# Two widths for the expert products: a branch on the expert's number of tokens chooses 224 or 256 columns

## The chip, the cores and the metric

The kernel runs on one core of one Trainium2 chip. The metric is the device time in microseconds (us) of one execution. TensorE's rows are named PE in the profile (PEld is its weight load), VectorE's DVE, ScalarE's ACT, GpSimd's POOL, and SyncE's SP. A "q" behind an engine's name marks its sequencer, the part that reads the program and hands instructions to the engine.

## The reference, cut to what matters

```python
def _moe_ref(x, w_gate, w1, w2, capacity):       # x: 1536 tokens of 512, from an attention
    expert_idx = np.argmax(x @ w_gate, axis=1)   # one of 8 experts for each token
    ...                                          # disp[e]: the tokens of expert e, capacity 384
    h = np.maximum(np.einsum('ecd,edf->ecf', disp, w1), 0.0)   # 512 -> 1024
    y = np.einsum('ecf,efd->ecd', h, w2)                       # 1024 -> 512
    ...                                          # out[i] = gate_w[i] * y[expert, position]
# reference: attention -> x -> _moe_ref -> SwiGLU of 512 -> 1536 -> 512
```

With the inputs that the reference draws, computing it gives 198, 119, 169, 188, 162, 192, 206 and 302 tokens for the experts 0 to 7.

## The kernel before

Three stages follow each other: the attention with the router (to about 284 us), the experts (to about 498 us), and the SwiGLU. The change is in the experts, in the class `Experts`.

`run` goes over the eight experts. The tokens of an expert are gathered as rows into `xr` by a DMA that ACT issues an expert ahead (the first by SP). `xt` turns two tiles of 128 tokens by transposes on TensorE (L839, tile `xp`) into `X`, 256 columns: a high part `Xh` (ACT, L842) and a rest `Xl` (DVE, L843). All products are made of such pairs, in three matmuls: high by high, high by rest, rest by high.

`l1` is called four times per expert. Each call fills one PSUM tile `hp` with 2 x 12 = 24 matmuls (L850) and evicts it: ACT writes `Hhh` with a Relu (L859), DVE the rest `Hhl` (L860). `l2` is called twice per expert; each call is 2 x 24 = 48 matmuls into `yp`, evicted to `Yh` (L870) and `Yl` (L871) at the column offset of the expert, which the engines hold in a register. An expert has so 4 x 24 + 2 x 48 = 192 matmuls, each with a weight load of its own; every one moves 256 columns, whatever the number of tokens.

An expert with more than 256 tokens has a third tile, in `over`, under a branch that all engines take by the register `cnt`; each engine loads it once per expert (L938), and the branch (L951) stands between the fourth `l1` and the transposes of the next expert:

```python
            cnt = ld(1, max_val=rt.CP) if nt > 2 else None
            ...
            for t in range(2, nt):
                with tc.If(cnt > t * 128):
                    self.over(e, t, off[t])
```

The order of the work on each engine is the order in the program. The weights come through four buffers `raw` (L807, SP's queue); `split` turns each into a high part (ACT, L816) and a rest (DVE, L817), in front of the calls of `l1` and `l2`. PSUM holds two `hp` and two `yp`, so that a product runs while the one before is evicted. Ahead of the first expert, 28 matmuls into an unused tile (L934) fill TensorE while the first rows are on their way; the first twelve of these have 192 columns.

Of the kernel before, what the change touches and what calls it, by code (L numbers as in the profile page):

```python
# [10 lines left out]
F32 = mybir.dt.float32  # L11
# [3 lines left out]
AF = mybir.ActivationFunctionType  # L15
ALU = mybir.AluOpType
# [749 lines left out]
class Experts:  # L766
# [43 lines left out]
    def split(self, e, i):  # L810
# [6 lines left out]
        nc.vector.tensor_tensor(out=l, in0=t, in1=h.bitcast(F32), op=ALU.subtract)  # L817
        self.load(8 * e + i + NRAW)

# [23 lines left out]
            nc.vector.tensor_tensor(out=X[1][:, ks, 0:n], in0=ps[:, :, 0:n], in1=X[0][:, ks, 0:n].bitcast(F32),  # L843
                                    op=ALU.subtract)

    def prod(self, out, W, ks, cols, mov):
        n, i = len(ks) * 3, 0
        for k in ks:
            for a, b in ((0, 0), (0, 1), (1, 0)):
                self.nc.tensor.matmul(out, lhsT=W[a][:, k, cols], rhs=mov[b][:, k, :], start=i == 0, stop=i == n - 1)  # L850
                i += 1

    def l1(self, mp, Hh, tag):
        nc = self.nc
        ps = self.ps.tile([128, 2, 256], F32, tag=tag, name="hp")
        for m in range(2):
            self.prod(ps[:, m], self.W1, range(self.KD), slice((2 * mp + m) * 128, (2 * mp + m + 1) * 128), self.X)
        ms = slice(2 * mp, 2 * mp + 2)
        nc.scalar.activation(out=Hh[0][:, ms], in_=ps, func=AF.Relu)  # L859
        nc.vector.scalar_tensor_tensor(out=Hh[1][:, ms], in0=ps, scalar=0.0, in1=Hh[0][:, ms].bitcast(F32), op0=ALU.max,  # L860
                                       op1=ALU.subtract)

    def l2(self, dp, Hh, off, n, tag):
        nc = self.nc
        ps = self.ps.tile([128, 2, 256], F32, tag=tag, name="yp")
        for m in range(2):
            self.prod(ps[:, m], self.W2, range(self.KF), slice((2 * dp + m) * 128, (2 * dp + m + 1) * 128), Hh)
        dsl = slice(2 * dp, 2 * dp + 2)
        y = [t[:, dsl, ds(off, n)] for t in self.Y]
        nc.scalar.copy(out=y[0], in_=ps[:, :, 0:n])  # L870
        nc.vector.tensor_tensor(out=y[1], in0=ps[:, :, 0:n], in1=y[0].bitcast(F32), op=ALU.subtract)  # L871

    def high_first(self, ks):

# [36 lines left out]
    def run(self, hook):  # L911
        nc, tc, rt = self.nc, self.tc, self.rt
        E, nt = self.E, self.nt
        ET = mybir.EngineType
        base = list(range(min(2, nt)))
        nb = 128 * len(base)
        if nb < 256:
            for t in self.X:
                nc.vector.memset(t.bitcast(F32), 0.0)
        self.rows(0, nc.sync)  # L920
        for k in range(self.KD):
            for t in self.Y:
                nc.gpsimd.memset(t[:, k].bitcast(F32), 0.0)
        for i in range(4):
            self.split(0, i)
        w = self.ps.tile([128, 2, 256], F32, tag="hp", name="hp").rearrange("p a b -> p (a b)")
        for i in range(14):
            nc.tensor.transpose(w[:, 0:128], self.ident, self.ident)
        rt.offsets(self.p1, self.ps.tile([128, 2, 256], F32, tag="xp", name="xp")[:, 0, 0:E])
        for i in range(24):  # L930
            nc.tensor.transpose(w[:, 0:128], self.ident, self.ident)
        for i in range(28):
            n = 512 if i > 11 else 192
            nc.tensor.matmul(w[:, 0:n], lhsT=self.W1[0][:, 0, 0:128], rhs=self.W1[0][:, 0, 0:n], start=True, stop=True)  # L934
        self.xt(0, base, "xp")
        for e in range(E):
            self.rows(e + 1)
            ld = lambda t, **k: nc.values_load(rt.offi[0:1, t, e:e + 1], min_val=0,  # L938
                                               skip_runtime_bounds_check_because="counts of tokens", **k)
            two = [ET.Activation, ET.DVE]  # L940
            off = {t: ld(t, engines=two, max_val=rt.N) for t in [0] + list(range(2, nt))}
            cnt = ld(1, max_val=rt.CP) if nt > 2 else None
            if e == 5:
                rt.hots([h[:, f] for h in self.Ho for f in range(self.KF)][:rt.B * rt.J], self.hs[:, 0:128])
            for mp in range(4):
                self.split(e, 4 + mp)
                self.l1(mp, self.Hh, "hp")
                if (e, mp) == (5, 3):
                    rt.tokens(self.ps.tile([128, 512], F32, tag="ov", name="xp")[:, 0:2 * rt.B * rt.J])
# [3 lines that stand above are left out]
            if e == 0:  # L953
                rt.ranks(self.p1)
                rt.invert(self.p1)
            if e + 1 < E:
                self.xt(e + 1, base, "xp")
            for dp in range(2):
                if e + 1 == E and dp:
                    hook(1)  # L960
                self.split(e + 1, 2 * dp)
                self.split(e + 1, 2 * dp + 1)
                if e + 1 == E and not dp:
                    hook(0)
                self.l2(dp, self.Hh, off[0], nb, "yp")
        hook(2)


class Glu:
# [51 lines left out]
    def convert(self, g, i):  # L1021
# [10 lines left out]
        v.scalar_tensor_tensor(out=b, in0=Hw, scalar=0xC0000000, in1=b, op0=ALU.bitwise_and, op1=ALU.bitwise_or)  # L1032
        v.scalar_tensor_tensor(out=m, in0=m, scalar=TINY, in1=b.bitcast(F32), op0=ALU.is_ge, op1=ALU.mult)  # L1033
        h, l = [w[:, i * 512:(i + 1) * 512] for w in self.sets[g % 2]]
        nc.scalar.copy(out=h, in_=m)  # L1035
        nc.gpsimd.tensor_tensor(out=l, in0=m, in1=h.bitcast(F32), op=ALU.subtract)  # L1036
        self.load(6 * g + i + NRAW)

# [72 lines left out]


NRAW = 4
TINY = 3.4332275390625e-05


@with_exitstack
def tile_clustered_attention_moe_swiglu(ctx, tc, q, k, v, cent, gate, w1, w2, wg, wv, wo, out, cap):
# [5 lines left out]
    const = ctx.enter_context(tc.tile_pool(name="const", bufs=1))  # L1124
    raw = ctx.enter_context(tc.tile_pool(name="rawp", bufs=NRAW))
    with tc.manual_schedule():
# [15 lines left out]
        with ExitStack() as c2:  # L1142
# [7 lines left out]
            with ExitStack() as c3:  # L1150
                ex = Experts(tc, c3, rt, w1, w2, ident, raw, W1, W2, Y)
                ex.next = glu.load
                for i in range(NRAW):
                    ex.load(i)
# [7 lines left out]
def dbg_attn(ctx, tc, q, k, v, cent, gate, xo, cap):  # L1162
# [4 lines left out]
    const = ctx.enter_context(tc.tile_pool(name="const", bufs=1))  # L1167
    raw = ctx.enter_context(tc.tile_pool(name="rawp", bufs=NRAW))
    with tc.manual_schedule():
# [41 lines left out]
```

## Time and profile before

| | |
|---|---|
| three runs | 803.13 us (median), 802.59 to 803.83 |
| the profiled execution | 802.74 us; span of its instructions 801.0 us |
| mean granted clock of TensorE | 0.995 of 2.4 GHz |
| PE busy | 776.8 us, 97% of the span |
| DVE, ACT, POOL busy | 529.3, 387.8, 191.8 us |
| matmuls with their weight loads | 4793 |

The profile is of one execution. A share of busy time near 100% says that an engine has something in hand, not that it runs at its best rate: matmuls overlap, so the distance between two starts counts, not the length of one. PEclk is the granted share of the TensorE clock: 1.0 is 2.4 GHz, 0.5 is 1.2 GHz. All times in rows are us from the start of the span.

### The profile page before, as it was taken

The numbers are of one execution on the slowest core, as the hardware profiler recorded it, in microseconds if no ns is written. First come the engines' busy times: TensorE is split into PE (matmuls) and PEld (weight loads), VectorE is DVE, ScalarE is ACT, GpSimd is POOL, SyncE is SP. The second block draws the span as 40 slices with busy tenths as digits, with TensorE's granted clock in tenths as the row PEclk, the third lists the DMA queues.
The fourth block names the chain that finished last, engine by engine and source line by source line (L and its number), as shares of the span: only waits on it lengthen the run. The fifth ranks groups of instructions, "written<-read, shape, count | busy, mean of one in ns | idle before, by whom it ended". The sixth has DMA issues, their size and how long they took to land. (4 is left out here: it accounts for less than half of the span.)

```text
span 801.0 us, 12679 instructions
## 1 busy us (share of the span) xinstructions
PE 776.8 (97%) x4793; PEld 652.8 (81%) x4793; DVE 529.3 (66%) x871; ACT 387.8 (48%) x704; POOL 191.8 (24%) x212
## 2 busy tenths in 40 slices
PE   7999999999999989999999999999999999999996
PEld 6777777777767789999999988778888888888885
DVE  5777777877877647565665644787766766676433
ACT  5777677777777535454554443354232232222210
POOL 6121121111211360000040001344333233323234
PEclk9999999999999989999999999999999999999999
DMA  9856966735541276656765641223121122210012
GB/s 203 198 119 198 220 173 180 178 81 118 139 155 40 80 262 198 196 192 211 234 202 191 194 126 54 82 99 109 54 80 52 55 78 66 66 54 1 0 53 105
DMA packets 93313, 102.03 MB, mean 127 GB/s; under 512 B 30304, under 2 KB 77408, under 8 KB 93248
## 3 DMA queue, kind: packets, MB, share of 16 engines
q1 hardware_dynamic: 88384, 89.33, 39.3%
q0 software_dynamic: 1920, 6.29, 2.1%
q10 hardware_dynamic: 2944, 5.54, 2.0%
q8 instruction: 41, 0.67, 0.3%
q14 instruction: 24, 0.20, 0.1%
HBM read 68.21 MB, written 12.58 MB: 101 GB/s over the span
## 5 line engine op out<-in xcount | busy, mean ns | idle before, releaser
L342 DVE TENSOR_REDUCE nm<-s 128x1 f32<-128x768 f32 x96 | 91.0, 949 | 12.1 <-PE s L339 10.5
L352 ACT ACTIVATE P<-s,nm 128x768 f32<-128x768 f32 x96 | 86.5, 901 | 13.4 <-DVE nm L342 10.4
L368 PE MATMUL t<-ident,P 128*128 128x128 f32 x576 | 81.2, 274 | 0.9 <-ACT PT L371 0.6
L368 PEld LDWEIGHTS t<-ident,P 128*128 128x128 f32 x576 | 68.5, 141 | 7.7 <-DVE PT L373 2.5
L850 PE MATMUL hp<-Xl,W1h 128*128 128x256 f32 x256 | 73.5, 287 | 0.1
L850 PE MATMUL hp<-Xh,W1h 128*128 128x256 f32 x256 | 73.5, 287 | 0.0
L850 PE MATMUL hp<-Xh,W1l 128*128 128x256 f32 x256 | 73.2, 286 | 0.0
L850 PE MATMUL yp<-Hhh,W2h 128*128 128x256 f32 x256 | 73.1, 285 | 0.0
L850 PE MATMUL yp<-Hhh,W2l 128*128 128x256 f32 x256 | 72.5, 283 | 0.0
L850 PE MATMUL yp<-Hhl,W2h 128*128 128x256 f32 x256 | 72.4, 283 | 0.0
L387 PE MATMUL acc<-PT,ldv 128*64 128x384 f32 x384 | 69.7, 495 | 0.0
L1063 POOL TENSOR_TENSOR ghl<-u,ghh 128x512 fp32r<-128x512 f32 x36 | 49.9, 1385 | 75.0 <-ACT ghh L1062 75.0
L339 PE MATMUL s<-Ak,Aq 128*128 128x384 f32 x192 | 58.5, 385 | 3.4 <-ACT P L352 3.2
L1082 DVE TENSOR_TENSOR acc<-o,acc 128x512 f32<-128x512 f32 x60 | 41.2, 691 | 31.0 <-PE o L1074 31.0
L1060 DVE TENSOR_TENSOR u<-sg,g 128x512 f32<-128x512 f32 x36 | 24.7, 687 | 54.0 <-ACT sg L1059 52.8
L371 ACT COPY PT<-t 128x384 f32<-128x384 f32 x96 | 45.8, 477 | 29.9 <-PE t L368 29.7
L1036 POOL TENSOR_TENSOR W1l<-cm,W1h 128x512 fp32r<-128x512 f32 x18 | 23.4, 1301 | 140.3 <-ACT W1h L1035 140.3
L1062 ACT CAST ghh<-u 128x512 fp32r<-128x512 f32 x36 | 22.4, 623 | 67.5 <-DVE u L1061 67.5
L373 DVE COPY PT<-t 128x384 f32<-128x384 f32 x96 | 52.3, 545 | 0.9 <-PE t L368 0.9
L339 PEld LDWEIGHTS s<-Ak,Aq 128*128 128x128 f32 x192 | 29.0, 189 | 28.3 <-ACT P L352 20.3
L339 PE MATMUL s<-kB,qB 80*128 80x384 f32 (+1 forms) x192 | 50.2, 341 | 1.5 <-DMA kB<-oT 0.8
L850 PEld LDWEIGHTS hp<-Xl,W1h 128*128 128x128 f32 x256 | 50.1, 196 | 0.4 <-DVE Xl L843 0.4
(269 smaller groups left out, 1972.0 us busy)
## 6 DMA issues: line engine op xcount, KB each, us to landing
raw<-in_moe_w SPq DMA_DIRECT2D x64, 512.0 KB, 4.2
Ak<-Hk SPq DMA_DIRECT2D x32, 192.0 KB, 4.8
moe_rows<-zero SPq DMA_DIRECT2D x8, 768.0 KB, 5.4
raw<-in_moe_w_gate SPq DMA_DIRECT2D x12, 512.0 KB, 3.6
raw<-in_moe_w_val SPq DMA_DIRECT2D x12, 512.0 KB, 3.5
raw<-in_moe_w_out SPq DMA_DIRECT2D x12, 512.0 KB, 3.4
xr<-moe_rows ACTq DMA_DIRECT2D x7, 768.0 KB, 6.1
ldq<-in_q SPq DMA_DIRECT2D x16, 192.0 KB, 4.2
```

The source lines that it names most:

```text
L339: nc.tensor.matmul(ps[:, c, 0:HS], lhsT=ql[:, qs], rhs=kr[:, c * HS:(c + 1) * HS], start=a == 0, stop=a == 1)
L342: nc.vector.tensor_reduce(out=nm, in_=ps[:, :, 0:HS], axis=AX.XY, op=ALU.max, negate=True)
L352: nc.scalar.activation(out=P, in_=ps[:, :, 0:HS], func=AF.Exp, bias=nm, accum_out=self.pairs[n]["sum"][:, i, r:r + 1])
L368: nc.tensor.transpose(ps[:, jj, :], P[:, a, jj * 128:(jj + 1) * 128], self.ident)
L371: nc.scalar.copy(out=PT[:, js, cs], in_=ps)
L373: nc.vector.tensor_copy(PT[:, js, cs], ps)
L387: nc.tensor.matmul(acc[c * D:(c + 1) * D], lhsT=v[:, c * HJ + j], rhs=PT[:, c * HJ + j, :], start=j == 0, stop=j == HJ - 1, tile_position= ...
L850: self.nc.tensor.matmul(out, lhsT=W[a][:, k, cols], rhs=mov[b][:, k, :], start=i == 0, stop=i == n - 1)
L1036: nc.gpsimd.tensor_tensor(out=l, in0=m, in1=h.bitcast(F32), op=ALU.subtract)
L1060: nc.vector.tensor_tensor(out=u, in0=sg, in1=ps[0], op=ALU.mult)
L1063: nc.gpsimd.tensor_tensor(out=hl[:, fc], in0=u, in1=hh[:, fc].bitcast(F32), op=ALU.subtract)
L1082: nc.vector.tensor_tensor(out=a, in0=p[t], in1=a, op=ALU.add)
```

## The change

`prod` gets a width `w`; `l1` and `l2` put their whole work, the tile, the matmuls and the two evictions, into a body that `arms` writes twice, under a branch on `cnt`: 256 columns above 224 tokens, 224 columns otherwise. `cnt` is loaded as before. The matmuls that fill TensorE ahead of the first expert become 26 of 512 columns.

```diff
-    def prod(self, out, W, ks, cols, mov):
+    def prod(self, out, W, ks, cols, mov, w):
...
-                self.nc.tensor.matmul(out, lhsT=W[a][:, k, cols], rhs=mov[b][:, k, :], start=i == 0, stop=i == n - 1)
+                self.nc.tensor.matmul(out[:, 0:w], lhsT=W[a][:, k, cols], rhs=mov[b][:, k, 0:w], start=i == 0, stop=i == n - 1)
...
+    def arms(self, body):
+        with self.tc.If(self.cnt > NARROW) as c:
+            body(256)
+        with c.Else():
+            body(NARROW)
+
     def l1(self, mp, Hh, tag):
...
+        def body(w):
+            ps = self.ps.tile([128, 2, 256], F32, tag=tag, name="hp")
+            for m in range(2):
+                self.prod(ps[:, m], self.W1, range(self.KD), slice((2 * mp + m) * 128, (2 * mp + m + 1) * 128), self.X, w)
+            ms = slice(2 * mp, 2 * mp + 2)
+            H, L = [h[:, ms, 0:w] for h in Hh]
+            nc.scalar.activation(out=H, in_=ps[:, :, 0:w], func=AF.Relu)
+            nc.vector.scalar_tensor_tensor(out=L, in0=ps[:, :, 0:w], scalar=0.0, in1=H.bitcast(F32), op0=ALU.max,
+                                           op1=ALU.subtract)
+        self.arms(body)
...
-        for i in range(28):
-            n = 512 if i > 11 else 192
-            nc.tensor.matmul(w[:, 0:n], lhsT=self.W1[0][:, 0, 0:128], rhs=self.W1[0][:, 0, 0:n], start=True, stop=True)
+        for i in range(26):
+            nc.tensor.matmul(w, lhsT=self.W1[0][:, 0, 0:128], rhs=self.W1[0][:, 0, 0:512], start=True, stop=True)
...
-            cnt = ld(1, max_val=rt.CP) if nt > 2 else None
+            cnt = self.cnt = ld(1, max_val=rt.CP)
...
+NARROW = 224
```

`l2` is changed in the same way, with `yp`, `W2` and the columns `ds(off, w)` of `Y`.

On TensorE, where the first call of `l1` of an expert meets the second, the program before has (`hp` is the PSUM tile, `Xh` and `Xl` the tokens, `W1h` and `W1l` the weights):

```order
L850 MATMUL hp<-Xh,W1h 128x256
L850 MATMUL hp<-Xl,W1h 128x256
L850 MATMUL hp<-Xh,W1l 128x256
L850 MATMUL hp<-Xh,W1h 128x256 [waits PE_49]
L850 MATMUL hp<-Xl,W1h 128x256
L850 MATMUL hp<-Xh,W1l 128x256
```

In the changed program the same place has the end of the narrow arm, then the branch of the second call and the head of its wide arm:

```order
L850 MATMUL hp<-Xh,W1h 128x224
L850 MATMUL hp<-Xl,W1h 128x224
L850 MATMUL hp<-Xh,W1l 128x224
L854 UNCONDITIONAL_BRANCH
L854 COMPARE_AND_BRANCH
L850 MATMUL hp<-Xh,W1h 128x256 [waits PE_49]
L850 MATMUL hp<-Xl,W1h 128x256
L850 MATMUL hp<-Xh,W1l 128x256
```

The wide arm stands first, the narrow one behind it: an expert with up to 224 tokens jumps over 24 wide matmuls with their weight loads (48 in `l2`) to reach its own. Between two groups stand an unconditional branch and a conditional one.

On ACT, after the split of a chunk of weights (L816), the changed program has both evictions of `hp`, each followed by a branch (DVE has the same pattern with its own eviction):

```order
L816 CAST W2h<-raw 128x4x256 [waits DMAHW2_49]
L854 COMPARE_AND_BRANCH
L868 ACTIVATE Hhh<-hp 128x512 [waits PE_49]
L854 UNCONDITIONAL_BRANCH
L868 ACTIVATE Hhh<-hp 128x2x224 [waits PE_49]
L854 UNCONDITIONAL_BRANCH
L816 CAST W2h<-raw 128x4x256 [waits DMAHW3_49]
```

Before, the eviction stood there once, directly between the two splits. SP and POOL have no work in the arms, but carry their branches too.

## Rows read from the trace of the kernel before

**Rows 1.** The page: TensorE and its clock in 40 slices.

```profile
PE   7999999999999989999999999999999999999996
PEclk9999999999999989999999999999999999999999
```

**Rows 2.** Window over one expert: busy time by engine, granted clock, DMA share, GB/s.

```profile
core 0: us, PE busy (x) PEld busy (x) DVE busy (x) ACT busy (x) POOL busy (x), PEclk, DMA share, GB/s
337.40:361.70 24.30, 24.15 (x203) 23.98 (x202) 14.96 (x16) 12.27 (x16) 0.00 (x0) 1.00 0.65 208
```

**Rows 3.** The chain that ended last: start us, length us, what.

```profile
448.53 11.52 PE yp L850 x96
530.86 2.72 PE v L1054 x12
```

**Rows 4.** Timeline of TensorE ahead of the first expert: start, length, what, idle before.

```profile
274.17 2.84 PE L931 MATMUL hp<-ident 128*128 128x128 f32 x24
276.76 5.24 PE L934 MATMUL hp<-W1h 128*128 128x192 f32 x28
284.63 1.97 PE L839 MATMUL xp<-ident,xr 128*128 128x128 f32 x8 [2.62 <-DMA xr<-moe_rows]
286.42 0.58 PE L850 MATMUL hp<-Xh,W1h 128*128 128x256 f32 x1
287.14 0.58 PE L850 MATMUL hp<-Xl,W1h 128*128 128x256 f32 x1
...
288.16 0.41 PE L850 MATMUL hp<-Xh,W1l 128*128 128x256 f32 x1
288.37 0.41 PE L850 MATMUL hp<-Xh,W1h 128*128 128x256 f32 x1
...
291.33 0.28 PE L850 MATMUL hp<-Xh,W1l 128*128 128x256 f32 x1
```

**Rows 5.** Timeline of TensorE, 277.2 to 277.8: eight matmuls of 192 columns.

```profile
276.94 1.05 PE L934 MATMUL hp<-W1h 128*128 128x192 f32 x8
```

**Rows 6.** Windows behind two idle times of TensorE, columns as in rows 2.

```profile
19.60:23.00 3.40, 3.37 (x25) 3.29 (x26) 2.02 (x3) 2.71 (x6) 0.41 (x1) 1.00 0.86 234
284.50:291.30 6.80, 6.53 (x28) 6.01 (x29) 2.61 (x3) 2.21 (x3) 6.80 (x5) 0.50 0.97 314
```

**Rows 7.** Timeline of TensorE: the longest idle time that the clock outlasted.

```profile
19.64 0.62 PE L339 MATMUL s<-Ak,Aq 128*128 128x384 f32 x2 [1.37 <-ACT P L352]
```

**Rows 8.** The line of the branch before, whole run: duration ns min/median/max, first, last start.

```profile
L951 PEldq COMPARE_BRANCH  x9: 70/322/388, 298.3 to 486.5; - x9
L951 ACTq COMPARE_BRANCH  x9: 38/45/50, 300.6 to 487.2; - x9
L951 PEldq EVENT_SEMAPHORE  x7: 51/51/51, 300.6 to 447.4; - x7
```

**Rows 9.** The same line on TensorE's sequencer, one skipped `over`, 320 to 326 us.

```profile
L951 PEldq COMPARE_BRANCH  x1: 328/328/328, 322.5 to 322.5; - x1
L951 PEldq EVENT_SEMAPHORE  x1: 51/51/51, 324.9 to 324.9; - x1
```

**Rows 10.** Timeline of TensorE at that place.

```profile
324.56 0.28 PE L850 MATMUL hp<-Xh,W1l 128*128 128x256 f32 x1
324.99 0.52 PE L839 MATMUL xp<-ident,xr 128*128 128x128 f32 x3
```

**Rows 11.** The load of `cnt` on TensorE's sequencer, all eight experts.

```profile
L938 PEldq TENSOR_LOAD <-offi x8: 299/308/494, 284.6 to 457.7; - x8
```

**Rows 12.** Timelines of ACT and DVE, two groups of `l1`.

```profile
319.62 1.04 ACT L816 CAST W2h<-raw 128x1024 fp32r<-128x1024 f32 x1
322.00 0.60 ACT L859 ACTIVATE Hhh<-hp 128x512 fp32r<-128x512 f32 x1 [1.35 <-PE hp L850]
322.63 0.69 DVE L860 SCALAR_TENSOR_TENSOR Hhl<-hp,Hhh 128x512 fp32r<-128x512 f32 x1 [0.72 <-ACT Hhh L859]
```

**Rows 13.** DMA queue of TensorE's program: kind, packets, MB, share of 16 engines.

```profile
q8 instruction: 41, 0.67, 0.3%
```

More of the change, by code (lines that the diff above doesn't have):

```diff
@@ L854, in l1 @@
         nc = self.nc
[L855 to L861, printed above, removed]
+        def body(w):
[7 more added lines that the diff above has]
+                                           op1=ALU.subtract)
@@ L863, in l2, with body @@
+        self.arms(body)
     def l2(self, dp, Hh, off, n, tag):
         nc = self.nc
[L865 to L871, printed above, removed]
+        def body(w):
+            ps = self.ps.tile([128, 2, 256], F32, tag=tag, name="yp")
+            for m in range(2):
+                self.prod(ps[:, m], self.W2, range(self.KF), slice((2 * dp + m) * 128, (2 * dp + m + 1) * 128), Hh, w)
+            dsl = slice(2 * dp, 2 * dp + 2)
+            y = [t[:, dsl, ds(off, w)] for t in self.Y]
+            nc.scalar.copy(out=y[0], in_=ps[:, :, 0:w])
+            nc.vector.tensor_tensor(out=y[1], in0=ps[:, :, 0:w], in1=y[0].bitcast(F32), op=ALU.subtract)
@@ L873, in high_first @@
+        self.arms(body)
     def high_first(self, ks):
```

## The prediction

> **What bounds the kernel now.** I read the page first: TensorE is at 9 tenths or more in nearly every slice, and its clock dips in one slice only [rows 1]. The window over one expert then says that it is TensorE alone that counts there: in 24.30 us PE is busy for 24.15, DVE for 14.96, ACT for 12.27, and the DMA engines for 0.65 of the time [rows 2]. The chain that ended last runs through the products of the experts and of the SwiGLU: 96 matmuls of `yp` take 11.52 us, 0.120 us from start to start [rows 3]. So what TensorE gains per matmul in the experts arrives at the end, unless something else takes its place.
>
> How far 0.120 us lies above the floor is read from other widths. Twelve matmuls of 512 columns take 2.72 us, 0.2267 each [rows 3]: 256 columns more cost 0.1067 us, which is 256 columns at 2.4 GHz, so a matmul takes its columns at 2.4 GHz and 0.0133 us more. By this line 224 columns would take 0.1066 us. But eight matmuls of 192 columns, which would take 0.093 by it, take 1.05 us [rows 5]: with some 0.28 for the last one that is 0.110 us each. And 24 transposes of 128 columns take 2.84 us [rows 4], with 0.28 for the last 0.111 each. Width no longer matters there: each has a weight load of 128 columns, and the loads come no faster. So 224 columns lie below the knee of the two lines (at some 235 columns), and go at the floor. I take 0.1115.
>
> The Trainium skill ("TensorE: Matmul & The Clock Gate", "Back-to-back issue gap") gives N / 2.4 + 2.5 ns for a single matmul, 13.3 ns less for 224 columns than for 256; by it the narrow arms would save 1344 x 13.3 ns = 17.9 us. Rows 5 speak against it. Its section on LDWEIGHTS gives columns / 1.2, 107 ns for 128, which is close to the floor of these rows.
>
> **The change part by part.** *Narrow matmuls.* Seven of eight experts have up to 224 tokens by the inputs; the trace agrees as far as it can: TensorE's sequencer met the extra wait of a skipped `over` seven times [rows 8]. Seven times 192 are 1344 matmuls. The first 22 of expert 0 are counted below with the clock; the other 1322 save 0.1200 - 0.1115 = 0.0085 us each: **-11.2 us**. Bounds: no gain at 0.1200 and -17.7 us at 0.1066; 224 lies as far from 192 as from 256, and I go by the flat stretch from 128 to 192.
>
> *Matmuls ahead of the first expert.* Twelve of 0.111 us and sixteen of 0.2267 become 26 of 0.2267, 0.9 us more. The 28 end at 282.00 and TensorE then sits idle for 2.62 us, until the rows land at 284.63 [rows 4]; so the 0.9 us fall into idle time, which shrinks to 1.7 us. What can change is the clock. It was at 0.50 (1.2 GHz) in the 6.8 us behind that idle time [rows 6]; an idle time of 1.37 us elsewhere [rows 7] was followed by a clock of 1.00 [rows 6]. 1.7 lies between, nearer to the one that was harmless, so I take it that the clock holds. At the low clock the matmuls of expert 0 stand 0.21 us apart (288.16, 288.37), and the 22nd starts at 291.33 [rows 4]. At the full clock four transposes, 0.11 apart instead of 0.21, are done some 0.5 us sooner, the first matmul starts at about 285.9 instead of 286.42, the second 0.72 later as now (it waits for `Xl`), and twenty more at 0.1115 bring the 22nd to 288.9: **-2.4 us**. If the clock falls all the same, these twenty go at 224 columns / 1.2 GHz, 0.187 instead of 0.213: -0.5 us.
>
> *Branches on TensorE.* Between two groups TensorE's sequencer now runs an unconditional branch and a conditional one that is taken. A branch has been there once per expert: taken it takes about 0.32 us, once, not taken, 0.07 [rows 8]. It does not hold the matmuls up by itself: it runs at 322.5, when the last matmul ahead of it starts only at 324.56 [rows 9, 10]; the sequencer is 2.0 us ahead. What delays the transposes to 324.99 is a wait of the skipped arm (324.9) for the last matmul [rows 9, 10], 0.31 us more than the distance of 0.12. The new arms have no such wait, since both hand out the same signals. So the cover is a lead of 2.0 us, against some 0.5 us for a pair of branches and, between experts, 0.31 for the load of `cnt` [rows 11]; 24 matmuls last 2.7 us, in which the sequencer can catch up. In the third and fourth `l1` the lead is shorter, because the group waits for the eviction two groups back: `Hhl` ends at 323.32 [rows 12], 1.6 us behind the start of its group's last matmul (321.68: a group of 24 x 0.12 ahead of 324.56) [rows 10], which leaves 1.1 us of the 2.7. That too covers a pair. The lead is nil once per expert, behind the wait at 324.9: eight transposes, 0.9 us, are all that covers the branch of `l2`. I charge 0.1 us there, seven times: **+0.7 us**; bounds 0 and 0.5 us each.
>
> *Branches elsewhere.* ACT takes at most 0.05 us for one [rows 8] and waits 1.35 us for TensorE at every group, DVE 0.72 us [rows 12]; 0.2 us less per group leaves both waiting. Their evictions become shorter. The weights of an expert must come in 22.7 us instead of 24.3 (192 x 0.0085 = 1.6 less), 223 GB/s by 208, with the DMA engines at 0.70 instead of 0.65 [rows 2]. Nothing here is on the path, and I charge nothing; if that cover were gone, each `l1` would pay two branches of ACT, 0.1 us.
>
> **Sum**, against the profiled execution's 802.74 us: 802.74 - 11.2 - 2.4 + 0.7 = 789.8. The median of the runs is 0.4 higher than the profiled one, so I give **790.1 us**.
>
> **The rivals.** *The clock falls again.* 1.7 us idle may be too long as 2.62 was. Then 2.4 becomes 0.5: 792.1 us.
>
> *The sequencer becomes the bound (slower).* A taken branch may cost more than its row shows: in the seven cases so far, the 2.0 us up to the wait hide whatever fetching the target took. The program of TensorE comes in 41 blocks of 16 KB [rows 13], 0.3% of 16 engines over 801 us, 0.9 us each. If the jump of every narrow group waits for such a block, a group costs 0.3 to 0.5 us of branches and 0.9 us of fetch, and the lead, once used up, is not built again. The gain of 13.6 us is gone at 13.6 / 42 = 0.32 us of stall per narrow group; at 0.6 us the time would be 790 + 42 x 0.6 = 815. Against it: the skipped `over` is a jump over 66 matmuls, the new jumps go over 24 or 48, and the wait behind it ran at 324.9, as soon as the last matmul (324.56 and 0.28 us long) had ended [rows 9, 10]; whatever the jump fetched was there by then. The Trainium skill ("Runtime: NRT & Kernel Launch", "Instruction fetch mechanics") says that a taken branch whose target lies outside the current two pages has to wait for a DMA, and calls it a reason to unroll; by it this rival holds only where a jump leaves both pages.
>
> *Part of this.* Stalls of 0.1 to 0.2 us per narrow group, because the weight load behind a branch is not drawn ahead: 794 to 799 us.
>
> *The widths don't tell.* If a matmul with these weight loads falls to the floor only near 192 columns, 224 gains nothing; the clock's 2.4 us less the 0.7 leave about 801.4, faster by 0.2%.
>
> **How the numbers follow.** The forecast gets 0.57, the falling clock 0.20, partial stalls 0.09, the useless width 0.03 and the sequencer 0.11. The forecast's own range is 788.0 to 791.5 (floor between 0.110 and 0.1125, stalls between 0 and 1.5 us); the falling clock adds up to 794, part of the partial stalls up to 796. Range 787.5 to 796. A measurement here tells 0.2%, 1.6 us, from no change. Faster by more: the first three cases and a part of the fourth, 0.87; slower 0.10; the same 0.03.
>
> **What the profile after would show.** Matmuls of 224 columns 0.1115 us apart in experts 0 to 6 and 0.120 in expert 7; an expert 22.7 us long instead of 24.3; the clock at 1.00 from 284 to 291 us; COMPARE_BRANCH rows on TensorE of about 0.3 us that end more than 1 us ahead of the matmul they lead to. The prediction is wrong if PE shows idle time behind the branches of most groups (then by the sequencer), if the 224-column matmuls stand 0.115 us apart or more, or if ACT's or DVE's waits for PE are gone.

## The result and the profile after

The changed kernel takes **791.4 us** (median of 4 runs, 789.09 to 793.73); the kernel before took 803.09 us beside it (802.59 to 803.83). The ratio is 0.9856, 95% interval 0.9836 to 0.9876: faster by 11.7 us. The profiled execution is the slowest of the four: 793.73 us, a span of 792.0 us. The four differ by TensorE's mean granted clock: 793.73 us at 0.989, 791.99 at 0.994, 790.81 at 0.997, 789.09 at 0.999.

The page of the changed kernel, which answers to [rows 1] and [rows 13]: TensorE, its clock, and the DMA queue of its program.

```profile
PE   8999999999999989999999999999999999999996
PEclk9899999999999999999999999999999999999998
q8 instruction: 54, 0.88, 0.5%
```

The dip of the clock in the 15th slice of before (8) is no longer visible at this grain; a new one stands in the second slice, in the attention, whose code was not touched. TensorE's program now comes in 54 packets instead of 41.

Windows over four stages, first of the changed kernel, then of the kernel before: up to the end of the filling matmuls, the idle time behind them, the experts (from the first transpose of `xr` to the first matmul of the SwiGLU), the rest. Columns as in [rows 2].

```profile
0.00:285.75 285.75, 276.96 (x1819) 209.86 (x1819) 208.98 (x449) 198.17 (x415) 60.70 (x95) 0.98 0.58 147
285.75:287.42 1.67, 0.00 (x0) 0.00 (x0) 0.00 (x0) 0.00 (x0) 1.67 (x2) 1.00 0.87 321
287.42:489.50 202.08, 198.37 (x1677) 193.93 (x1677) 121.74 (x153) 98.70 (x136) 22.00 (x23) 0.99 0.62 200
489.50:792.00 302.50, 294.88 (x1298) 242.75 (x1296) 193.89 (x269) 88.83 (x153) 107.34 (x95) 0.99 0.20 64
```

```profile
0.00:282.01 282.01, 271.29 (x1821) 204.08 (x1821) 209.92 (x447) 198.06 (x415) 59.84 (x94) 1.00 0.59 148
282.01:284.63 2.62, 0.00 (x0) 0.00 (x1) 0.29 (x3) 0.00 (x0) 2.62 (x3) 0.96 0.87 312
284.63:498.49 213.86, 210.61 (x1676) 205.97 (x1677) 125.22 (x153) 100.96 (x136) 21.97 (x23) 0.98 0.58 189
498.49:801.00 302.51, 294.87 (x1298) 242.76 (x1296) 193.87 (x269) 88.79 (x153) 107.35 (x95) 1.00 0.19 63
```

The experts are 11.8 us shorter (213.86 to 202.08), the SwiGLU is as long as before. The stretch ahead of the experts is 3.74 us longer, of which 0.9 is the longer fill; the fill takes that back out of the idle time (2.62 to 1.67). What is left, 2.8 us, was lost in the attention, as windows of the changed kernel show (same columns):

```profile
9.00:13.00 4.00, 4.00 (x24) 4.00 (x24) 3.02 (x9) 1.37 (x3) 2.60 (x2) 0.59 0.96 202
17.00:20.00 3.00, 1.58 (x6) 1.01 (x6) 2.73 (x4) 2.70 (x5) 1.05 (x8) 1.00 0.97 213
20.00:23.50 3.50, 3.15 (x13) 3.06 (x14) 1.28 (x3) 1.65 (x5) 0.00 (x0) 0.50 0.81 222
23.50:26.50 3.00, 3.00 (x14) 2.90 (x14) 1.33 (x2) 2.23 (x5) 1.00 (x1) 0.50 0.90 196
289.70:293.00 3.30, 3.30 (x17) 3.30 (x17) 0.87 (x2) 1.05 (x1) 3.30 (x3) 0.50 1.07 369
293.10:300.00 6.90, 6.90 (x64) 6.90 (x63) 4.37 (x6) 3.62 (x6) 3.28 (x5) 1.00 0.95 320
```

The clock is at 0.50 (1.2 GHz) in most of the first window (from 9.74 us on), from 20 to 26.5 us, and again from 289.7 to 293.0. Behind the first of these stretches the same matmuls start 0.7 us later than in the kernel before, behind the second 2.8 us later. The second begins within the idle time that the next timeline shows ahead of 20.35: it is the 1.37 us that the kernel before outlasted in its profile [rows 6, 7].

TensorE's timeline of the changed kernel at the same three places as [rows 4], [rows 7] and [rows 10], with the chain's row for one expert's `yp` at the end:

```profile
20.35 1.01 PE L339 MATMUL s<-Ak,Aq 128*128 128x384 f32 x2 [1.37 <-ACT P L352]
...
287.42 1.09 PE L839 MATMUL xp<-ident,xr 128*128 128x128 f32 x8 [1.68 <-DMA xr<-moe_rows]
288.76 0.37 PE L850 MATMUL hp<-Xh,W1h 128*128 128x224 f32 x1 [0.24 <-ACT Xh L842]
289.48 0.45 PE L850 MATMUL hp<-Xl,W1h 128*128 128x224 f32 x1 [0.36 <-DVE Xl L843]
289.73 0.42 PE L850 MATMUL hp<-Xh,W1l 128*128 128x224 f32 x1
...
293.44 0.27 PE L850 MATMUL hp<-Xh,W1h 128*128 128x224 f32 x1
293.55 0.27 PE L850 MATMUL hp<-Xl,W1h 128*128 128x224 f32 x1
...
324.35 0.27 PE L850 MATMUL hp<-Xh,W1l 128*128 128x224 f32 x1
324.77 1.06 PE L839 MATMUL xp<-ident,xr 128*128 128x128 f32 x8
325.59 0.35 PE L850 MATMUL yp<-Hhh,W2h 128*128 128x224 f32 x1
...
440.32 10.71 PE yp L850 x96
```

Four things are to be read here. The matmuls of 224 columns stand 0.11 us apart (293.44, 293.55), and 96 of them take 10.71 us, 0.1116 each, where 11.52 stood [rows 3]. The first eight transposes go at the full clock (1.09 us instead of 1.97), but then the clock falls and the matmuls are 0.21 us apart until 293. Behind a skipped `over` the transposes come 0.42 us after the last `hp` matmul, as before (0.43 in [rows 10]). And `yp` follows the eight transposes without an idle time, though a branch lies between.

The window over one expert and the new line of the branches, of the changed kernel; these answer to [rows 2] and [rows 8]:

```profile
336.39:359.04 22.65, 22.50 (x203) 22.34 (x201) 14.50 (x16) 11.97 (x16) 0.00 (x0) 1.00 0.68 220
```

```profile
L854 PEldq COMPARE_BRANCH  x54: 65/212/472, 288.0 to 487.4; - x54
L854 ACTq COMPARE_BRANCH  x54: 34/45/50, 291.4 to 489.7; - x54
L854 DVEq COMPARE_BRANCH  x54: 43/56/72, 292.5 to 490.3; - x54
```

An expert takes 22.65 us instead of 24.30, and PE is still idle for 0.15 us of it alone. The 54 branches of TensorE are one for each of the 42 narrow groups and two for each of the six wide groups of expert 7: a narrow group runs one branch, not the pair that the prediction charged.

### The profile page after: what moved, and what is told of

Same layout as the page of the kernel before. It is cut to its first block, busy times and chain, and to the rows that moved or that the text cites. A ratio compares the mean times of both kernels' runs of the same rounds, so it can differ in the third digit from the quotient of the medians.

```text
span 792.0 us, 12961 instructions
## 1 busy us (share of the span) xinstructions
PE 770.2 (97%) x4791; PEld 646.5 (82%) x4791; DVE 524.6 (66%) x871; ACT 385.7 (49%) x704; POOL 191.7 (24%) x212
## 3 DMA queue, kind: packets, MB, share of 16 engines
q0 software_dynamic: 1920, 6.29, 2.1%
## 5 line engine op out<-in xcount | busy, mean ns | idle before, releaser
L850 PE MATMUL hp<-Xl,W1h 128*128 128x224 f32 (+1 forms) x256 | 71.4, 279 | 0.4 <-DVE Xl L843 0.4
L850 PE MATMUL hp<-Xh,W1h 128*128 128x224 f32 (+1 forms) x256 | 71.3, 279 | 0.2 <-ACT Xh L842 0.2
L850 PE MATMUL hp<-Xh,W1l 128*128 128x224 f32 (+1 forms) x256 | 71.3, 278 | 0.0
L850 PE MATMUL yp<-Hhh,W2h 128*128 128x224 f32 (+1 forms) x256 | 71.1, 278 | 0.0
L850 PE MATMUL yp<-Hhh,W2l 128*128 128x224 f32 (+1 forms) x256 | 70.5, 275 | 0.0
L850 PE MATMUL yp<-Hhl,W2h 128*128 128x224 f32 (+1 forms) x256 | 70.5, 275 | 0.0
```

What stands on the lines that cost most here:

```text
L850: self.nc.tensor.matmul(out[:, 0:w], lhsT=W[a][:, k, cols], rhs=mov[b][:, k, 0:w], start=i == 0, stop=i == n - 1)
```

## The experiments

"Stage" is the time from the first transpose of `xr` to the first matmul of the SwiGLU in the profiled execution; "first group" is the time from that transpose to the 24th `hp` matmul (7.05 us before, 6.24 after). Each ratio is to runs of the kernel before on the same chip. What was open was where the 11.7 us come from: from the narrower matmuls, from the fill, or less something that the branches cost.

### One part at a time: e1, e2, e3, e4

e1 is the changed kernel with the old fill; e2 is the kernel before with the new fill; e3 has both arms, each with 256 columns, and the old fill; e4 has none of the new branches, 224 columns for every expert, and the new fill.

```diff
 e1, against the changed kernel
-        for i in range(26):
-            nc.tensor.matmul(w, lhsT=self.W1[0][:, 0, 0:128], rhs=self.W1[0][:, 0, 0:512], start=True, stop=True)
+        for i in range(28):
+            n = 512 if i > 11 else 192
+            nc.tensor.matmul(w[:, 0:n], lhsT=self.W1[0][:, 0, 0:128], rhs=self.W1[0][:, 0, 0:n], start=True, stop=True)
 e2, against the kernel before: the same lines the other way round
 e3, against e1
         with c.Else():
-            body(NARROW)
+            body(256)
 e4, against the changed kernel
     def arms(self, body):
-        with self.tc.If(self.cnt > NARROW) as c:
-            body(256)
-        with c.Else():
-            body(NARROW)
+        body(NARROW)
```

Expected of e1: 

> The two arms, with the fill of before (12 matmuls of 192 columns, 16 of 512). If the floor of the weight loads is the gain and the branches are hidden, 1322 narrow matmuls save 0.0083 us each: 11.0 us, and some 0.4 us in the low clock of expert 0, so 791.7 us; the expert stage lasts 202.0 to 203.0 us. If the longer fill carries a part of the gain (the rival, 2.4 us by the prediction), this kernel stays 0.8 to 2.4 us above the change.

Expected of e2: 

> The longer fill alone, no arms. If the clock holds behind an idle time of 1.7 us, 800.7 us and a granted clock of 1.00 in the first product of expert 0; if it falls all the same, 802.3 to 803.1 us.

Expected of e3: 

> All branches of the change, with 256 columns in both arms and the fill of before: the branches alone. If they are hidden by the lead of TensorE's sequencer, 803.1 us within 0.3%. If they cost 0.1 to 0.3 us per group that the narrow arms paid for, 48 groups make it 808 to 817 us.

Expected of e4: 

> 224 columns for every expert, no branch (leaves out the columns 224 to 255 of expert 7). If the branches cost nothing, only expert 7's 192 matmuls gain: 192 x 0.0083 = 1.6 us, so 789.8 us by the change's 791.4, and an expert takes 22.65 us as in the change. If the branches cost 0.1 us per group, 4.8 us more: 785.

| kernel | median us (range) | ratio (95%) | stage | first group |
|---|---|---|---|---|
| e1, arms only | 795.05 (793.16 to 799.01) | 0.9898 (0.9873 to 0.9922) | 207.17 | 6.90 |
| e2, fill only | 802.73 (800.13 to 805.01) | 0.9987 (0.9973 to 1.0002) | 213.12 | 6.29 |
| e3, both arms wide | 804.83 (800.35 to 807.09) | 1.0007 (0.9991 to 1.0022) | 214.23 | 6.92 |
| e4, no branch | 789.12 (786.54 to 791.45) | 0.9820 (0.9793 to 0.9848) | 200.27 | 6.14 |

All the branches at the old width change nothing that can be measured (e3). The fill alone brings 0.7 us by the medians and at most 2.2 by the interval (e2). The gain comes from the width. e4's stage is 1.8 us under that of the changed kernel; 192 matmuls of expert 7 at 0.0083 us less are 1.6 of it, which leaves 0.2 us for all branches together. By e3's stage, with the old width, it is 0.4 us over that of the kernel before. e1 missed what was expected of it: its median of 795.05 us lies above 791.7 and above the 792.2 to 793.8 of its rival. Its stage, too, is 5.1 us over that of the changed kernel, where the fill explains some 0.7 (the first group), and its profile shows why. TensorE and, under it, the branch line, of e1:

```profile
325.87 0.27 PE L850 MATMUL hp<-Xh,W1l 128*128 128x224 f32 x1
326.29 1.06 PE L839 MATMUL xp<-ident,xr 128*128 128x128 f32 x8
329.21 0.37 PE L850 MATMUL yp<-Hhh,W2h 128*128 128x224 f32 x1 [1.86 <-ACT Xh L842]
329.42 0.27 PE L850 MATMUL yp<-Hhl,W2h 128*128 128x224 f32 x1
...
330.32 0.42 PE L850 MATMUL yp<-Hhh,W2l 128*128 128x224 f32 x1
330.54 0.41 PE L850 MATMUL yp<-Hhh,W2h 128*128 128x224 f32 x1
```

```profile
L854 PEldq COMPARE_BRANCH  x1: 2823/2823/2823, 326.3 to 326.3; - x1
```

The profile names `Xh` of ACT as what ended the 1.86 us. That is a wrong trail: in the changed kernel this `yp` starts at 325.59, before that `Xh` has begun (326.03). What did end there is the branch, at 326.33 + 2.82 = 329.15. It stands behind the skipped `over` of expert 1, the place that the prediction had named as the one without a lead. The idle time then cost the clock too: 330.1 to 333.4 at 0.50, with matmuls 0.21 us apart.

### What the long branch waits for: e8, e9, e11

A first idea was that the branch's cost depends on where its target lies in the 16 KB blocks of the program, and that the two filling matmuls which e1 has more had moved it. e8 has the fill of e1 with two matmuls fewer, e9 the new fill cut into two more, and e11 is e1 again.

```diff
 e8, against e1
-        for i in range(28):
-            n = 512 if i > 11 else 192
+        for i in range(26):
+            n = 512 if i > 9 else 192
 e9, against the changed kernel
-        for i in range(26):
-            nc.tensor.matmul(w, lhsT=self.W1[0][:, 0, 0:128], rhs=self.W1[0][:, 0, 0:512], start=True, stop=True)
+        for i in range(28):
+            n = 512 if i > 3 else 256
+            nc.tensor.matmul(w[:, 0:n], lhsT=self.W1[0][:, 0, 0:128], rhs=self.W1[0][:, 0, 0:n], start=True, stop=True)
```

Expected of e8: 

> The arms alone again, with the fill 10 x 192 + 16 x 512 instead of 12 x 192 + 16 x 512: two matmuls fewer in front of everything that follows, so that TensorE's later instructions stand where they stand in the changed kernel. In the arms alone (795.1 us) one branch at L854, behind the skipped over of expert 1, took 2823 ns with a 16 KB transfer of instructions of 961 ns begun inside it, and TensorE stood 1.86 us and then ran 3.5 us at 0.50. Theory: what that branch costs depends on where its target lies in the blocks that are fetched, so that moving the code by two matmuls moves it away. Then no branch of L854 is over 1000 ns, no gap over 0.4 us inside the experts, the expert stage is 202 to 203.5 us instead of 207.2, and the time 791.5 to 793. Rival: the stall comes from the short fill itself (its later start or its clock). Then it stays at expert 1, 207 us, 795.

Expected of e9: 

> The changed kernel with its fill of the same 13312 columns cut into 24 x 512 + 4 x 256: two matmuls more, nothing else (some 0.03 us of time). Theory of the place of the code: expert 1's branch at L854 behind the skipped over again takes about 2.8 us, TensorE stands near 1.9 us there and loses its clock for some 3 us; the expert stage grows from 202.1 by 3 to 5 us and the time is 794.5 to 796.5. Rival (the short fill was the cause): no stall, 791.4 within 0.3%.

Expected of e11: 

> The arms alone once more, unchanged, for a second profile. Theory that the late packet is a chance of the execution: the 2823 ns branch of expert 1 is gone or at another expert, the 16 KB packets start at the same places of the program (within 40 instructions or so), and without a stall the expert stage is 203 to 204 us. Rival that it belongs to this program: again over 2000 ns at expert 1, stage near 207.

Measured: e8 793.21 us (792.61 to 793.93), ratio 0.9870 (0.9852 to 0.9889), stage 203.50. e9 792.54 (790.16 to 795.32), 0.9867 (0.9845 to 0.9889), stage 201.33. e11, one execution: 793.92 us, stage 202.96. So the idea falls: e9's program has as many instructions ahead of each place as e1's, and no idle time there; e8's branch, which should have stayed under 1000 ns, took 1235; e11 is e1's own program, and its branch at that place took 730 ns with no idle time behind it. So the stall comes in some executions of the same program and not in others. How often isn't shown: of e1's six runs one has a profile, the slowest (799.01 us), and runs of 797.66 and 796.02 us have none. Without the stall the arms alone are worth what was expected: e11's stage is 10.9 us under that of the kernel before, which has the same fill.

What it waits for can be read from the packets of TensorE's program queue. For the branch behind the skipped `over` of expert 1, in us, worked out from the records of the trace (the branch of the `over`, the next 16 KB packet's start and length, the branch of `l2` and its length, and how far that ends behind the packet's end):

```
kernel    over     packet          l2 branch        end behind packet's end
e9        319.55   319.61 + 1.02   321.89 + 0.42    1.69
changed   322.48   322.56 + 0.96   324.82 + 0.42    1.71
e11       322.51   322.90 + 1.33   324.86 + 0.73    1.36
e8        320.94   322.19 + 0.96   323.28 + 1.24    1.36
e1        323.99   326.84 + 0.96   326.33 + 2.82    1.35
```

The packet is the 20th of the queue in all five, at the same place of the program. Where it came within 0.1 us of the skipped `over`, the branch takes its 0.42 us; the later it starts, the longer the branch, up to a constant 1.36 us behind the packet's end. In the eleven profiles with arms 20 branches of TensorE took more than 0.48 us, and all 20 end 1.33 to 1.65 us behind the end of such a packet. Most lie under TensorE's work ahead of them; e1's of 2.82 us did not, and e8's of 1.24 us left 0.27 us idle. The Trainium skill ("Runtime: NRT & Kernel Launch", "Instruction fetch mechanics") says that a taken branch whose target lies outside the two pages at hand has to wait until the target's page is fetched. The trace agrees in so far as each of the 20 long branches follows a packet; in which page a target lies, it doesn't show. Here the fetch was nearly always done in time.

### Why the packet starts late, and whether another order of the arms helps: e10, e12

```diff
 e10, against the changed kernel (spare is a new tensor in memory, 512 x 512)
+            for j in range(4):
+                nc.sync.dma_start(out=rt.spare[j * 128:(j + 1) * 128, :], in_=rt.zero)
             if e + 1 < E:
                 self.xt(e + 1, base, "xp")
 e12, against the changed kernel
-        with self.tc.If(self.cnt > NARROW) as c:
-            body(256)
-        with c.Else():
-            body(NARROW)
+        with self.tc.If(self.cnt < NARROW + 1) as c:
+            body(NARROW)
+        with c.Else():
+            body(256)
```

Expected of e10: 

> The changed kernel with four more transfers of 256 KB for each expert, from the zero tile to memory that nothing reads, issued by SyncE around the time of the skipped over. Theory that the fetch of instructions starts late because it waits among data transfers: with 1 MB more in flight there, the packet behind the skipped over starts 1 to 3 us behind that branch at most experts (0.06 to 1.25 us so far, 2.85 in the one stall), branches at L854 of over 1000 ns appear at two or more experts, and TensorE stands 0.5 to 2 us behind some of them: 793 to 800 us. Rival that the start is not set by data traffic: starts of 0.1 to 1.3 us and branches under 1000 ns stay; weights that land up to 4 us later may then stall TensorE at an hp or yp matmul, with a DMA as the releaser and no long branch.

Expected of e12: 

> The changed kernel with its two arms in the other order: the test is count below 225, the 224 columns stand first and are run into, and the jump over the 256 columns comes behind the arm instead of ahead of it. In the traces so far the branch behind a skipped over ends about 1.36 us after the 16 KB packet of instructions that it needs has ended (e8: packet 322.19 + 0.96, branch to 324.51; e9: 301.82 + 1.12, to 304.35; arms alone: 326.84 + 0.96, to 329.15), and takes 0.42 us where the packet was early. Theory: the two jumps in a row (66 matmuls, then 48, with eight transposes between) are what outruns the fetch; with the arm between them the test takes 65 to 70 ns at every l2, none over 600, and time is that of the changed kernel or up to 1 us less: 790.4 to 791.6. Rival: the jump behind the last hp arm now stands directly ahead of the skipped over, so the long branch only moves to there (L963 or the jump's own place) and a stall is as likely as before: same time, branches over 600 ns at L963.

e10, one execution: 793.86 us, stage 202.67. Its branch line, and e12's at both places:

```profile
L854 PEldq COMPARE_BRANCH  x54: 65/213/2110, 287.5 to 487.4; - x54
```

```profile
L854 PEldq COMPARE_BRANCH  x90: 67/176/924, 286.5 to 479.0; - x90
L963 PEldq COMPARE_BRANCH  x9: 73/225/1766, 297.3 to 474.7; - x9
```

In e10 one branch took 2.11 us, between the two halves of an `l2` and behind a packet that started at 373.08, 1.4 to 2.8 us after four of the added transfers were issued (370.3 to 371.6), and took 1.49 us; the matmuls ahead covered it but for 0.02 us. The theory wanted this at two or more experts, with idle time behind, and that isn't there (the next longest, 977 ns at expert 6, has its like in kernels without the added transfers, 954 ns in e5); at expert 1 the added transfers were issued at 325.0, too late to meet the packet of 322.5. So data traffic as the reason for the late start is neither shown nor excluded. e12: 790.23 us (789.11 to 793.59), ratio 0.9845 (0.9819 to 0.9871), which overlaps that of the changed kernel. The test of the narrow arm now takes 67 to 73 ns at the `l2` behind each skipped `over`, but the longest branch appears at the `over` of expert 2 (1766 ns, no idle time), as the rival had it; another, of 924 ns, is the jump ahead of the fourth `l1` of expert 0, where the theory wanted none over 600. Without its first group, whose clock held (below), e12's stage is 196.35 us long, that of the changed kernel 195.84: the other order doesn't help.

What fits a late packet also stands away from a branch. In e9 and in e6 (below) TensorE stood still in the middle of a run of `yp` matmuls, with nothing to wait for. Timeline of TensorE in e6:

```profile
390.69 0.28 PE L850 MATMUL yp<-Hhh,W2l 128*128 128x240 f32 x1
392.25 0.38 PE L850 MATMUL yp<-Hhh,W2h 128*128 128x240 f32 x1 [1.28 <-issue]
```

"issue" means that the profile shows no wait. The 16 KB packet there started at 389.76, 0.16 us behind a branch of `l2` that took 0.21 us, and ended at 390.64, 1.6 us ahead of the matmul, about as far as the long branches end behind theirs. In e9 the packet of the same expert ended at 389.82 (388.11 + 1.71) and the matmul that followed started at 391.38, 0.66 us late. So such idle times stand in four of the eleven profiles with arms (e1 1.86 us, e6 1.28, e9 0.4, e8 0.27), and in none of the three without (before, e2, e4).

### The floor by width: e5 and e6

```diff
 e5, against the changed kernel
-            body(NARROW)
+            body(192)
 e6, against the changed kernel
-NARROW = 224
+NARROW = 240
```

Expected of e5: 

> The narrow arm computes 192 columns instead of 224 while the threshold stays 224, so columns 192 to 223 of the experts with more than 192 tokens are left out. Theory of a floor (a matmul with weights of its own doesn't go under the load of its weights, 0.1115 us): spacing 0.1117 us as with 224 columns, time 791.4 within 0.2%. Rival (time by columns): 32 columns less are 0.0133 us less on each of 1322 narrow matmuls, 773.8 us; by the page's formula of columns and a constant the spacing would be 0.0825 to 0.093.

Expected of e6: 

> Both the threshold and the narrow arm at 240 columns. By the line through 256 and 512 columns (0.1200 and 0.2267 us, so columns / 2.4 GHz + 13.3 ns) 240 columns take 0.1133 us, over the floor of 0.1117: 1322 x 0.0016 = 2.1 us more than the changed kernel, 793.5 (if expert 7 stays wide). Rival that the floor is for 224 and fewer only because of a step in size: 0.1200, 802 us. Rival that the floor is higher than the line up to 255 columns: 0.1117, 791.4.

e5: 792.46 us (791.44 to 798.13), ratio 0.9882 (0.9851 to 0.9914). e6: 792.64 us (791.42 to 793.60), 0.9871 (0.9843 to 0.9899). The medians tell little at this size; the chain's row for 96 `yp` matmuls, which [rows 3] show for before, tells it directly. Of e5, then of e6:

```profile
437.97 10.70 PE yp L850 x96
```

```profile
438.87 10.76 PE yp L850 x96
```

At 192 columns 96 matmuls take as long as at 224 (10.70 and 10.71 us): the floor. At 240 they take 10.76, 0.1121 each: neither the 0.1133 that the line through 256 and 512 columns gives nor one of the rivals' values. So the time is nearly flat up to 240 and rises by 0.008 between 240 and 256, more steeply than by columns. In time this is some 0.0006 us for each of 1344 matmuls, 0.8 us: the stages, 200.35 us (e5) and 202.54 (e6), differ by about that and by the idle time shown above (390.69 to 392.25 is 1.56 us from start to start instead of 0.11, so 1.45).

### The fill once more: e7

```diff
 e7, against the changed kernel
-        for i in range(26):
+        for i in range(34):
```

Expected of e7: 

> The changed kernel with 34 x 512 instead of 26 x 512 in the fill: 8 x 0.2267 = 1.8 us more work in an idle time of 1.67 us in front of the first xt. Theory that the idle time lowers the clock: idle under 0.2 us, clock 1.00 through the first group, xt to the last matmul of the first group about 4.7 us instead of 6.24, less 0.15 for the longer fill: 790.0 us. Rival that the clock falls for another reason: 3.4 us at 0.50 stay and the time is 791.6. By the place of the code (eight matmuls more) one branch may also stall, which adds 1 to 5 us and shows as a branch of over 2000 ns.

TensorE's timeline and a window of e7:

```profile
281.74 4.47 PE L946 MATMUL hp<-W1h 128*128 128x512 f32 x19
286.05 1.08 PE L839 MATMUL xp<-ident,xr 128*128 128x128 f32 x8
287.37 0.37 PE L850 MATMUL hp<-Xh,W1h 128*128 128x224 f32 x1 [0.24 <-ACT Xh L842]
288.09 0.37 PE L850 MATMUL hp<-Xl,W1h 128*128 128x224 f32 x1 [0.36 <-DVE Xl L843]
288.30 0.27 PE L850 MATMUL hp<-Xh,W1l 128*128 128x224 f32 x1
```

```profile
285.00:292.00 7.00, 6.41 (x50) 5.62 (x49) 1.94 (x3) 2.82 (x5) 7.00 (x6) 1.00 0.99 332
```

Without idle time the clock stays at 1.00 and the first group takes 4.60 us. The time is 793.24 us (790.91 to 795.67), ratio 0.9874 (0.9854 to 0.9893): no better than 26 matmuls. The first group of all profiles, by the idle time ahead of it:

```
idle us        profiles                              clock behind it       first group us
2.57 to 2.83   before, e1, e3, e8, e11               0.50 for 6.8 us       6.90 to 7.13
1.65 to 1.73   changed, e2, e4, e10                  0.50 for 3.4 us       6.14 to 6.29
1.65 to 1.69   e5, e6, e9, e12                       1.00                  4.59 to 4.63
none           e7                                    1.00                  4.60
```

An idle time of 2.6 us or more lost the clock five times of five, one of 1.7 us four times of eight. The 1.37 us in the attention, which the prediction called harmless on the one profile it had, stand in twelve of the other profiles too (1.36 to 1.37 us), and in all twelve the clock goes to 0.50 for 3.4 or 6.8 us, from at most 0.84 us ahead of their end to 0.16 us behind it. That they are the cause isn't shown: in e7, the thirteenth, the idle time there is 0.79 us, and the clock is at 0.50 from 17.5 us on, ahead of it. That the prediction's profile of before is the odd one fits the runs of the kernel before, 800.5 to 805.5 us: 38 of the 45 beside the experiments have a mean clock below the 0.995 of that profile.

## Why the prediction came out right

**Narrow matmuls.** Forecast 0.1115 us each, measured 0.1116; 1322 of them save 1322 x 0.0083 = 11.0 us, where 11.2 stood. The floor between 128 and 192 columns reaches up to 224 (e5) and nearly to 240 (e6); the knee that the prediction put at some 235 columns lies above that. Shown by e3, e4 and e11: with the same branches and the old width nothing is gained, without them and with the new width all of it and expert 7's 1.6 us more, and with the old fill the stage loses 10.9 us.

**The fill and the clock.** The size was right where the clock held: 7.05 to 4.60 us is 2.45, forecast 2.4 (the start at 291.33, which the prediction calls the 22nd, is the 21st in the trace; counted rightly its working gives 2.6). Where it fell, 0.8 was gained, where 0.5 stood in that rival. But the profiled execution is one in which it fell, and so were half of those with the same idle time, so that the step was mis-sized: on the average of these eight, about 1.6 us instead of 2.4. Its ground failed, a single idle time of 1.37 us that the clock outlasted. That 11.0 + 0.8 = 11.8 us, which is what the stage lost (213.86 to 202.08), leaves nothing that can be seen for other causes in it.

**Branches on TensorE.** Forecast +0.7, measured 0 in the profile of the changed kernel: `yp` follows the transposes at 325.59 without idle time, and e4 leaves 0.2 us for all of them. The place was right, the price not: a narrow group runs one branch (207 to 472 ns in the changed kernel) instead of a pair, and it costs not 0.1 us each time but mostly nothing, and once in a while 0.3 to 1.9 us, with more behind it where the clock falls (e1's stage against e11's: 4.2 us). So the rival of the sequencer has its mechanism, TensorE waiting for a packet of its program, but not its frequency: it needed 0.32 us at each of 42 narrow groups, and there is at most one such idle time in a profile.

**Branches elsewhere.** As forecast: ACT still waits for TensorE at an `l1` group, 1.20 us where [rows 12] show 1.35, as the timeline of ACT in the changed kernel shows; its branches take at most 0.05 us, and the DMA share of an expert is 0.68.

```profile
321.98 0.55 ACT L868 ACTIVATE Hhh<-hp 128x448 fp32r<-128x448 f32 x1 [1.20 <-PE hp L850]
```

**The sum.** The profiled execution came out at 793.73 us rather than 789.8, because of 2.8 us of low clock in the attention, which the change doesn't touch, 1.6 in the first group, and -0.7 + 0.2 in the other terms. In the medians 791.4 stands against 790.1. That the two are so close is in part luck: the 0.7 us charged for branches, which cost next to nothing, made up for most of the 0.8 us by which the clock's term was too large.

## What to carry to other kernels

Before a matmul is made narrower, find the width at which its time stops falling: two widths on the slope and two on the floor, all from one trace, gave 0.0085 us per matmul (measured 0.0083) where the slope alone promises 0.0133. Here a branch was free as long as the engine had more work ahead of it than the branch and the packet behind it took; look for the place where a wait has just emptied that queue, and for idle time put down to "issue". A clock that survived an idle time in one profile has survived it once: take several profiles before a term of the sum rests on it.

## What was not expected of the hardware

- A taken branch on TensorE whose packet of instructions is late ends 1.33 to 1.65 us behind that packet's end, in 20 branches; otherwise it takes 0.17 to 0.47 us, and 0.07 not taken.
- The packet of the same place of the program starts between 0.06 and 2.85 us behind the skipped `over` in five profiles, 0.39 and 2.85 in two of one and the same program (e11, e1). What delays it stays open.
- The clock behind an idle time of 1.7 us fell in four profiles and held in four. What decides it stays open.
- A matmul with a weight load of its own takes 0.1116 us at 192 and at 224 columns, 0.1121 at 240 and 0.1200 at 256.
